# Moving the small q and output copies of a decode attention kernel from GpSimd to VectorE, with outputs laid out by tile

## The chip, the cores and the metric

The kernel runs on one core of one Trainium2 chip. The metric is device time in microseconds (us) from launch to end. The six runs of the kernel before span 0.22% (653.43 to 654.88 us), so differences below 0.3% are only read from repeated runs on the same chip. The trace of an execution starts and ends a little inside the device time: 652.1 us of trace belong to 653.5 us of time. A run counts as slow when it lies over 1.5% above the fastest of its kernel.

## The reference, cut to what matters

One decode step for 4 sequences: layer norm, grouped-query attention over a long cache, a gated MLP branch, and a residual.

```python
B, Sq, D = 4, 1, 448
Hq, Hkv, Sk, Dh = 16, 8, 8192, 256            # k_cache, v_cache: (B, Hkv, Sk, Dh), bfloat16
q = (x @ wq).reshape(B, Sq, Hq, Dh) ...
p = softmax(einsum(q, k) * Dh ** -0.5)
s = (p @ v) ... .reshape(B, Sq, Hq * Dh) @ wo
return x + s * g                              # g: silu of a small MLP (w3, w4)
```

The two caches are 4 x 8 x 8192 x 256 x 2 bytes = 134 MB each, and each element is used once. That is nearly all of the 279 MB that the kernel reads.

## The kernel before

Work goes in 32 tiles, one for each pair of a sequence and a key head (`NH = Bn * HKV`). For each tile one 4 MB transfer brings keys and one brings values. TensorE (PE) transposes the keys, VectorE (DVE) and ScalarE (ACT) copy the transposes to on-chip memory (SBUF), PE multiplies with q, then comes the softmax, and two tiles later the product with the values. Both caches are double buffered.

The loads go through one queue, in program order, and each waits until VectorE has said that its buffer is free:

```python
def where(h):
    return Bn - 1 - h // HKV, h % HKV          # batch 3 first, batch 0 last

def load_k(h):
    b, g = where(h)
    if h >= 2:
        sp.wait_ge(S["v_k"], h - 1)            # VectorE: keys of tile h-2 are used up
    sp.dma_start(kn_dst(h), A_k_cache[b, g]...)
def load_v(h):
    ...
    if h < NH - 1:
        sp.wait_ge(S["v_v"], h + 1)            # VectorE: values of tile h-2 are used up
        sp.dma_start(vflat[h % 2], ...)
...
for h in range(2, NH):
    load_k(h)
    load_v(h - 2)
```

GpSimd feeds q to each tile and puts each output in its place. Its addresses are Python constants, as its program is unrolled; VectorE runs a hardware loop of two tiles and so writes to `otmp` first:

```python
OT = sb("OT", [P, HKV, REP, NHALF, PQ], BF16)  # batch innermost: 32 columns lie side by side

def put(h):                                    # GpSimd
    b, g = where(h)
    gp.wait_ge(S["v_o"], h + 4)
    gp.tensor_copy(OT[:, g, :, :, b], otmp[:, h % 2]...).then_inc(S["g_p"], 1)
    ...
for h in range(NH):
    b, g = where(h)
    if h >= 2:
        gp.wait_ge(S["v_v"], h - 1)
    gp.tensor_copy(qc[:, h % 2], qT[:, b, g]).then_inc(S["g_q"], 1)
    if h >= 5:
        put(h - 5)
```

VectorE's end of a tile, and the output projection of the tail, which takes OT as PE weights:

```python
v.sem_inc(S["v_k"], 1)                         # keys free
f_rmax(h)                                      # row maximum; PE then transposes it
f_diag(h)                                      # global maximum, to PE
f_po(h - 2)                                    # first: v.sem_inc(S["v_v"], 1), values free

ins = pe.matmul(o_ps[...], OT[:, hq // REP, hq % REP, dh, :], wo_sb[...], ...)
```

The last pieces of `wo` are loaded after all keys and values, so the projection ends the kernel. `f_warm` matmuls, whose results are not used, fill PE's gaps in the tail.

Of the kernel before, what the change touches and what calls it, by code (L numbers as in the profile page):

```python
# [10 lines left out]
BF16 = dt.bfloat16  # L11

P = 128
# [42 lines left out]
def bass_recurrent_scan__gqa_block_cached__mixer_s_mlp__decode_kernel(  # L56
# [13 lines left out]
    Bn, Sq, D = A_x.shape  # L70
    _, HKV, SK, DH = A_k_cache.shape
    HD = A_wq.shape[1]
    HQ = HD // DH
    REP = HQ // HKV
# [11 lines left out]
    DQ, PQ = D // NDG, P // NQD  # L86
# [3 lines left out]
    NHALF = DH // P  # L90
    NKC = HD // P
    NH = Bn * HKV
# [20 lines left out]
    NLATE = sum(len(g) for g in LATE)  # L113
    NWARM = 14
    ROW_PAD = 192
    QW = HDH // NQD
    assert QW <= 512 and QW % P == 0 and NQC == NQD * (QW // P)

# [2 lines left out]


    def where(h):
        return Bn - 1 - h // HKV, h % HKV

    with ExitStack() as es:
        def sb(name, shape, dty):
            return es.enter_context(nc.sbuf_tensor(name, shape, dty))

        align = sb("align", [P, ROW_PAD], BF16)  # L130
        kn = sb("kn", [P, 2, NCH, DH], BF16)
# [3 lines left out]
        ident_f = sb("ident_f", [P, P], F32)  # L135
        ident_b = sb("ident_b", [P, P], BF16)
        ones_f = sb("ones_f", [P, P], F32)
        qT = sb("qT", [P, Bn, HKV, NHALF, REP], BF16)
        qc = sb("qc", [P, 2, NHALF, REP], BF16)
        otmp = sb("otmp", [P, 2, NHALF, REP], BF16)  # L140
        OT = sb("OT", [P, HKV, REP, NHALF, PQ], BF16)
        ou_f = sb("ou_f", [P, D], F32)
        selb = sb("selb", [P, PQ], F32)
        q_b = sb("q_b", [P, QW], BF16)
        pT = sb("pT", [P, 2, NCH * REP + PVW], BF16)
# [9 lines left out]
        rz = sb("rz", [P, 2, REP], F32)  # L155
# [25 lines left out]
        S = {n: es.enter_context(nc.semaphore(n)) for n in (  # L181
            ["dx", "dwq", "dw3", "dw4", "dwo", "dk0", "dk1", "dv0", "dv1", "dout", "pause"]
            + ["dvl%d" % i for i in range(NPIECE)] + ["dwl%d" % i for i in range(len(LATE))]
            + ["p_td", "p_ta", "p_sc", "p_m1", "p_m2", "p_m3", "p_tr", "p_ou", "p_pv", "p_x", "p_q", "p_h", "p_h2", "p_o"]
            + ["v_ev", "a_ev", "v_rmax", "v_diag", "v_neg", "v_ot", "a_exp", "g_q", "g_c",
               "v_s", "v_a", "v_qb", "p_qt", "v_h2", "p_hs", "v_k", "v_v", "v_po", "v_o", "g_o", "g_p", "g_f", "v_xT", "v_qT", "v_hT", "v_c", "v_w", "a_c", "v_out"])}


        vflat = [vb[:, i].rearrange("p c d -> p (c d)") for i in range(2)]
# [13 lines left out]
        o_ps = pst[0]  # L203
        ou_ps = pst[3]
        ol_ps = pst[1]

        def kn_dst(h):
            return kn[:, h % 2].rearrange("p c d -> p (c d)")
# [63 lines left out]
        def take(eng, name, n=1):  # L272
            return eng.wait_ge(S[name], n).then_inc(S[name], -n)  # L273

        NPI, NPC = 4, 12

        def prog_pool(gp):
            def put(h):
                b, g = where(h)
                gp.wait_ge(S["v_o"], h + 4)  # L280
                gp.tensor_copy(OT[:, g, :, :, b],
                               otmp[:, h % 2].rearrange("p dh r -> p r dh")
                               ).then_inc(S["g_p"], 1)
                gp.wait_ge(S["g_p"], h + 1)
                gp.sem_inc(S["g_o"], 1)

            c = _Chain(gp, S["g_c"])
            c(gp.memset(ident_f[:, :], 0.0))
            c(gp.memset(ident_b[:, :], 0.0))
            c.sync()  # L290
            for t in (ident_b, ident_f):
                c(gp.affine_select(out=t[:, :], in_=t[:, :], compare_op=ALU.not_equal, fill=1.0,
                                   base=0, pattern=[[-1, P]], channel_multiplier=1))
            c(gp.memset(ones_f[:, :], 1.0))
            c(gp.memset(diag[:, :], 0.0))
            c(gp.memset(sel[:, :, :].rearrange("p c n -> p (c n)"), 0.0))
            c(gp.memset(rz[:, :, :].rearrange("p s r -> p (s r)"), 1.0))
            gp.wait_ge(S["v_c"], 2)
            c(gp.memset(pT[:, :, :].rearrange("p s n -> p (s n)"), 0.0))
            for i in range(2):  # L300
                c(gp.memset(po[:, i], 0.0))
            c(gp.memset(OT[:].rearrange("p g r d b -> p (g r d b)"), 0.0))
            assert c.n == NPC
            gp.wait_ge(S["v_qT"], 1)
            for h in range(NH):
                b, g = where(h)
                if h >= 2:
                    gp.wait_ge(S["v_v"], h - 1)
                gp.tensor_copy(qc[:, h % 2], qT[:, b, g]).then_inc(S["g_q"], 1)  # L309
                if h >= 5:  # L310
                    put(h - 5)
            for h in range(NH - 5, NH - 3):
                put(h)
            gp.wait_ge(S["g_p"], NH - 3)
            gp.sem_inc(S["g_f"], 1)

        def evac(engine, h, j):
            take(engine, "p_td" if j in D_GROUPS else "p_ta")
# [44 lines left out]
        def prog_dve(v):  # L363
            c = _Chain(v, S["v_c"])
# [59 lines left out]
                c(v.memset(t[:, :], 0.0))  # L424
            c.sync()
            v.sem_inc(S["v_po"], 1)
            v.sem_inc(S["g_o"], 5)
            v.sem_inc(S["dv0"], 16)
            v.sem_inc(S["dv1"], 16)
            v.wait_ge(S["g_c"], NPC)  # L430
# [22 lines left out]
            for m in range(NQD):  # L453
                hh, dh = divmod(m, NHALF)
# [2 lines left out]
                    qt_ps[:, m * P:(m + 1) * P].rearrange("p (i n) -> p i n", i=NQD)[  # L457
                        :, :, 0:NHF * Bn].rearrange("p i (a b) -> p i a b", a=NHF)))
            c.sync()
            v.sem_inc(S["v_qT"], 1)  # L460
            v.wait_ge(S["a_c"], 5)
            c(v.tensor_scalar(gel_b[:, :], gel_b[:, :], 1.0, 0.5, op0=ALU.add, op1=ALU.mult))
            c.sync()
# [15 lines left out]
            def f_rmax(h):  # L479
                take(v, "p_sc")  # L480
                v.tensor_reduce(rmax[:, :], psc[h % 2][:, 0:NCH * REP].rearrange(  # L481
                    "p (k h) -> p h k", h=REP), AX.X, ALU.max).then_inc(S["v_rmax"], 1)

            def f_diag(h):
                take(v, "p_m1")
                v.tensor_reduce(gmax[:, :], psm[0:REP, 0:P], AX.X, ALU.max  # L486
                                ).then_inc(S["v_s"], 1)
                take(v, "v_s")
                v.tensor_scalar(diag[:, :], ident_f[0:REP, 0:REP], gmax[:, 0:1], -SCALE,
                                op0=ALU.mult, op1=ALU.mult).then_inc(S["v_diag"], 1)  # L490
# [7 lines left out]
                v.sem_inc(S["v_v"], 1)  # L498
                v.tensor_copy(po[:, slot], psv[:, 0:CP * DH]).then_inc(S["v_po"], 1)  # L499

            def f_ot(h, last=False, slot=0):
                o = P + (4 + slot * NHALF) * REP
                ot_src = psm[:, o:o + NHALF * REP].rearrange("p (a r) -> p a r", a=NHALF)
                b, g = where(h)
                dst = OT[:, g, :, :, b].rearrange("p r a -> p a r") if last else otmp[:, h % 2]
                v.tensor_tensor(dst, ot_src,
                                rz[:, h % 2, :].unsqueeze(1).broadcast_to([P, NHALF, REP]),
                                ALU.mult).then_inc(S["v_s"], 1)
                take(v, "v_s")

            def f_fin(h):
                take(v, "p_m3")
                take(v, "g_o")
                f_ot(h - 2)
                v.reciprocal(rz[:, h % 2, :], psm[:, P + REP:P + 2 * REP]
                             ).then_inc(S["v_s"], 1)
                take(v, "v_s")
                v.sem_inc(S["v_o"], 1)

            with nc.Fori(0, NH // 2, engines=[mybir.EngineType.DVE]):  # L520
                for h in range(2):
                    for j in range(NGR):
                        if j in D_GROUPS:
                            evac(v, h, j)
                        if j == J_BC + 1:
                            f_negb(h - 1)
                        if j == J_SUM + 2:
                            f_fin(h - 1)
                    v.sem_inc(S["v_k"], 1)
                    f_rmax(h)  # L530
                    f_diag(h)
                    f_po(h - 2)
            h = NH - 1
            f_negb(h)
            take(v, "p_m3")
            f_ot(h - 2, True)
            v.reciprocal(rz[:, h % 2, :], psm[:, P + REP:P + 2 * REP]).then_inc(S["v_s"], 1)
            take(v, "v_s")
            v.sem_inc(S["v_ot"], 1)
            f_po(h - 1, 1)  # L540
            take(v, "p_tr")
            f_ot(h - 1, True, 1)
            v.sem_inc(S["v_ot"], 1)
            take(v, "p_ou")
            v.tensor_copy(ou_f[:, :], ou_ps[:, 0:D]).then_inc(S["v_a"], 1)
# [1 line left out]
            b, g = where(h)  # L547
# [12 lines left out]
        def prog_pe(pe, xn_mark, xn2_mark):  # L560
# [60 lines left out]

            def f_s(h, j):
                if j == 0:
                    take(pe, "g_q")
                take(pe, "v_ev" if j in D_GROUPS else "a_ev")
                for t in range(TB):
                    kl, half = divmod(t, NHALF)
                    kk = GC * j + kl
                    ins = pe.matmul(psc[h % 2][:, kk * REP:(kk + 1) * REP],  # L629
                                    kT[:, j % RING, t * P:(t + 1) * P], qc[:, h % 2, half, :],  # L630
                                    start=(half == 0), stop=(half == NHALF - 1))
                if j == NGR - 1:
                    ins.then_inc(S["p_sc"], 1)
# [57 lines left out]
            h = NH - 1  # L691
# [40 lines left out]
            def finish():  # L732
                f_bc(h)
                take(pe, "dwo", 16)
                pe.wait_ge(S["g_f"], 1)
                f_ou(range(NLATE, HQ - 3 * REP))
                take(pe, "v_po")
                f_warm(4)
# [106 lines left out]
```

## Time and profile before

| | before |
|---|---|
| time, median of 6 runs | 653.65 us (653.43 to 654.88) |
| read from HBM | 279 MB, 428 GB/s over the span |
| queue q1 | 99.5% of the time of 16 DMA engines |
| busy share: PE, DVE, ACT, GpSimd | 85%, 42%, 39%, 2% |

From the page of the kernel before: busy us with share of the span; the clock granted to PE and the busy share of the DMA in 40 equal slices (9 is 90% or more); the queue. PEld is PE's loading of weights, POOL is GpSimd.

```profile
PE 553.9 (85%) x9937; PEld 473.0 (73%) x9937; DVE 274.7 (42%) x589; ACT 256.3 (39%) x364; POOL 13.7 (2%) x77
...
PEclk9699999887899888789977979897789988878989
DMA  9999999999999999999999999999999999999997
...
q1 hardware_dynamic: 12328, 278.99, 99.5%
```

Every slice but the last is full. A packet of 32,768 bytes takes 1.21 us in the packet records, and 16 of them run at a time: 433 GB/s. The other engines are less full. PE is busy 85% of the span and idle for 98 us; the next view shows that most of this is one wait.

The waits of the kernel before (engine, line, what ended the wait: total us, times, longest), and those of the load queue:

```profile
PEld pst L617 <- issue: 82.8, 30, 4.7
...
DVE gmax L486 <- DVEq L273: 35.6, 32, 2.0
```

```profile
SPq L232 <- DVEq L529: 458.2, 30, 38.3
SPq L240 <- DVEq L498: 133.6, 31, 18.0
```

L617 is the transposing of keys: PE stands still before it 30 times, 2.8 us on the mean, and 28 of these waits end 0.1 us after a key load has landed. ("issue" only says that the profile shows no releaser.) The load queue (SPq, the engine that issues the loads) waits for VectorE most of the time, but that does not mean that the DMA starves. The issue table (size, median us from issue to landing) answers that:

```profile
kn<-in_A_k_cache_dram SPq DMA_DIRECT2D x32, 4096.0 KB, 25.6
vb<-in_A_v_cache_dram SPq DMA_DIRECT2D x31, 4096.0 KB, 30.8
```

A 4 MB load needs 9.7 us at 433 GB/s but lands 25.6 us after its issue: the rest is earlier work in the queue.

GpSimd's groups (count, busy us, mean ns), and the end of the timeline (start us, us, and in brackets the idle time before):

```profile
L309 POOL COPY qc<-qT 128x4 bf16<-128x4 bf16 x32 | 5.9, 188 | 583.7 <-DVEq L498 568.2 <-DVEq L460 15.5
L281 POOL COPY OT<-otmp 128x4 bf16<-128x4 bf16 x29 | 5.9, 202 | 30.9 <-DVEq L518 30.9
```

```profile
648.24 0.91 PEld L716 LDWEIGHTS pst<-wo_sb,OT 128*32 128x32 bf16 x20 [0.38 <-issue]
...
649.38 0.14 PEld L716 LDWEIGHTS pst<-wo_sb,OT 128*32 128x32 bf16 x4 [0.23 <-issue]
```

So GpSimd does 12 us of copies in 652 us, and the output projection (L716) waits 0.23 us for the last piece of `wo` before its last four weight loads.

### The profile page before, as it was taken

To read this page: it belongs to the slowest core of one execution; us is meant where nothing else is said; L and a number is where in the kernel's file an instruction comes from. 1 tells how busy PE (TensorE), PEld (TensorE's weight loads), DVE (VectorE), ACT (ScalarE), POOL (GpSimd) and SP (SyncE) were. 2 spreads that over 40 slices of the span, in tenths; PEclk is the share of its full clock that TensorE was granted. 3 is DMA by queue.
4 is the path that set the end of the run, shared out by engine and by line. 5 is a ranking of instruction groups with operands and counts; after the bars stand their busy time and mean duration, and the time that the engine had idled before them with its cause. 6 is when DMAs were issued, how large, how long until landed. Compare 5 with 4: busy or idle time off the path is not lost. (4 is left out here: it accounts for less than half of the span.)

```text
span 652.1 us, 22855 instructions
## 1 busy us (share of the span) xinstructions
PE 553.9 (85%) x9937; PEld 473.0 (73%) x9937; DVE 274.7 (42%) x589; ACT 256.3 (39%) x364; POOL 13.7 (2%) x77
## 2 busy tenths in 40 slices
PE   2798997988888988888898878997888898888898
PEld 1476886876766887676787757777776698767685
DVE  7343554443443443344433434443344344334442
ACT  4143454443433444333443423444343344333340
POOL 2000000000000000000000000000000000000000
PEclk9699999887899888789977979897789988878989
DMA  9999999999999999999999999999999999999997
GB/s 375 441 416 440 425 440 428 438 428 436 432 424 444 422 446 420 446 422 444 424 440 428 440 426 440 424 440 428 430 438 426 442 424 444 424 442 426 440 425 299
DMA packets 12354, 279.14 MB, mean 428 GB/s; under 512 B 1204, under 2 KB 3256, under 8 KB 3768
## 3 DMA queue, kind: packets, MB, share of 16 engines
q1 hardware_dynamic: 12328, 278.99, 99.5%
q8 instruction: 7, 0.11, 0.1%
q14 instruction: 3, 0.02, 0.0%
q10 hardware_dynamic: 16, 0.01, 0.0%
HBM read 278.99 MB, written 0.00 MB: 428 GB/s over the span
## 5 line engine op out<-in xcount | busy, mean ns | idle before, releaser
L617 PE MATMUL pst<-ident_b,kn 128*128 128x128 bf16 x4096 | 344.9, 238 | 77.8 <-PEq L273 75.4
L324 ACT ACTIVATE kT<-pst 128x1024 bf16<-128x1024 bf16 x224 | 229.5, 1025 | 358.8 <-ACTq L273 357.8
L617 PEld LDWEIGHTS pst<-ident_b,kn 128*128 128x128 bf16 x4096 | 274.2, 107 | 83.5 <-issue 82.8
L322 DVE COPY kT<-pst 128x1024 bf16<-128x1024 bf16 x288 | 197.5, 692 | 260.2 <-DVEq L273 260.2
L629 PE MATMUL psc<-qc,kT 128*128 128x2 bf16 x4096 | 177.9, 164 | 0.0
L629 PEld LDWEIGHTS psc<-qc,kT 128*128 128x128 bf16 x4096 | 156.5, 97 | 28.5 <-issue 28.3
L668 PE MATMUL psv<-vb,pT 128*4 128x512 bf16 x1056 | 87.2, 381 | 1.4 <-issue 1.4
L647 PE MATMUL psm<-sel,po 128*128 128x2 f32 x272 | 36.8, 257 | 0.5 <-PEq L273 0.5
L647 PEld LDWEIGHTS psm<-sel,po 128*128 128x128 f32 x272 | 34.8, 196 | 0.9 <-issue 0.9
L668 PEld LDWEIGHTS psv<-vb,pT 128*4 128x4 bf16 x1056 | 22.3, 82 | 16.8 <-issue 2.5
L481 DVE TENSOR_REDUCE rmax<-psc 128x2 f32<-128x128 f32 x32 | 9.3, 292 | 49.9 <-DVEq L273 49.9
L499 DVE COPY po<-psv 128x512 f32<-128x512 f32 x34 | 23.5, 692 | 3.0 <-DVEq L273 2.3
L486 DVE TENSOR_REDUCE gmax<-psm 2x1 f32<-2x128 f32 x32 | 8.9, 279 | 35.6 <-DVEq L273 35.6
L346 ACT ACTIVATE pT<-psc,negb 128x64 bf16<-128x64 f32 x66 | 20.7, 333 | 5.4 <-ACTq L273 5.4
L641 PEld LDWEIGHTS psm<-diag,ones_f 2*128 2x128 f32 x66 | 13.9, 260 | 6.4 <-issue 5.2
L309 POOL COPY qc<-qT 128x4 bf16<-128x4 bf16 x32 | 5.9, 188 | 583.7 <-DVEq L498 568.2
L641 PE MATMUL psm<-diag,ones_f 2*128 2x2 f32 x66 | 16.6, 318 | 1.1 <-PEq L273 0.9
L346 ACT ACTIVATION_READ_ACCUMULATOR pT<-psc,negb 128x1 f32 x66 | 13.6, 206 | 0.0
L637 PEld LDWEIGHTS psm<-ident_f,rmax 128*2 128x2 f32 x32 | 2.6, 80 | 14.4 <-issue 14.4
L659 PE MATMUL psm<-rowsum,ones_f 128*128 128x2 f32 x64 | 11.6, 251 | 0.0
L565 PE MATMUL pst<-ident_b,xn_b 4*128 4x4 bf16 x14 | 0.6, 161 | 11.3 <-DVE xn_b L394 6.7
L659 PEld LDWEIGHTS psm<-rowsum,ones_f 128*128 128x128 f32 x64 | 9.5, 188 | 0.0
(101 smaller groups left out, 111.0 us busy)
## 6 DMA issues: line engine op xcount, KB each, us to landing
kn<-in_A_k_cache_dram SPq DMA_DIRECT2D x32, 4096.0 KB, 25.6
vb<-in_A_v_cache_dram SPq DMA_DIRECT2D x31, 4096.0 KB, 30.8
vb<-in_A_wq_dram SPq DMA_DIRECT2D x1, 3584.0 KB, 11.3
vb<-in_B_w_dram SPq DMA_DIRECT2D x2, 1568.0 KB, 16.2
wo_sb<-in_A_wo_dram SPq DMA_DIRECT2D x1, 2688.0 KB, 43.4
kn<-in_A_v_cache_dram SPq DMA_DIRECT2D x1, 2048.0 KB, 25.9
kn<-in_A_v_cache_dram SPq DMA_DIRECT2D x1, 1024.0 KB, 27.9
kn<-in_A_v_cache_dram SPq DMA_DIRECT2D x2, 512.0 KB, 29.1
```

The source lines that it names most:

```text
L322: engine.tensor_copy(dst, src).then_inc(S["v_ev"], 1)
L324: engine.activation(dst, src, ACT.Copy).then_inc(S["a_ev"], 1)
L346: ins = act.activation(pv_p[:, :, hh], sc[:, :, hh], ACT.Exp, bias=negb[:, s, hh:hh + 1], scale=SCALE, accum_out=rowsum[:, s, hh:hh + 1])
L481: v.tensor_reduce(rmax[:, :], psc[h % 2][:, 0:NCH * REP].rearrange("p (k h) -> p h k", h=REP), AX.X, ALU.max).then_inc(S["v_rmax"], 1)
L486: v.tensor_reduce(gmax[:, :], psm[0:REP, 0:P], AX.X, ALU.max).then_inc(S["v_s"], 1)
L499: v.tensor_copy(po[:, slot], psv[:, 0:CP * DH]).then_inc(S["v_po"], 1)
L617: ins = pe.transpose(dst[:, t * P:(t + 1) * P], kn[:, h % 2, GC * j + kl, half * P:(half + 1) * P], ident_b[:, :])
L629: ins = pe.matmul(psc[h % 2][:, kk * REP:(kk + 1) * REP], kT[:, j % RING, t * P:(t + 1) * P], qc[:, h % 2, half, :], start=(half == 0), st ...
L641: pe.matmul(psm[:, P:P + REP], ones_f[0:REP, :], diag[:, :], start=True, stop=True).then_inc(S["p_m2"], 1)
L647: ins = pe.matmul(dst(dh)[:, 0:width], po[:, slot, i * DH + dh:(i + 1) * DH:NHALF], sel[:, i, 0:width], start=(i == 0), stop=(i == CP - 1))
L659: pe.matmul(psm[:, P + REP:P + 2 * REP], ones_f[:, :], rowsum[:, h % 2, :], start=True, stop=True)
L668: ins = pe.matmul(psv[o:o + CP * REP, 0:CP * DH], pT[:, h % 2, kk * REP:(kk + CP) * REP], src[:, kk:kk + CP, :].rearrange("p c d -> p (c d)"),
```

## The change

GpSimd is taken out of the loop. VectorE's loop counts in elements (`at`), and its instructions address OT and q through that register. OT is laid out by tile and batches run from 0 up, so that the loop's one counter steps evenly through both q and OT. The intent is fewer hand-overs between engines: one operation in place of a write to `otmp`, a semaphore and a GpSimd copy.

```diff
     def where(h):
-        return Bn - 1 - h // HKV, h % HKV
+        return h // HKV, h % HKV
...
-        otmp = sb("otmp", [P, 2, NHALF, REP], BF16)
-        OT = sb("OT", [P, HKV, REP, NHALF, PQ], BF16)
+        OT_all = sb("OT_all", [P, OT_AHEAD * TW + PQ * HKV * TW], BF16)
...
+        OT = OT_all[:, OT_AHEAD * TW:].rearrange("p (b g d r) -> p g r d b", g=HKV, d=NHALF, r=REP)
...  (GpSimd: put(h) and the loop over tiles removed)
-            v.sem_inc(S["v_qT"], 1)
+            v.tensor_copy(qc[:].rearrange("p s d r -> p (s d r)"), qT_all[:, 0:2 * TW]
+                          ).then_inc(S["v_q"], 2)
...
+            def f_q(at, s):
+                v.tensor_copy(qc[:, s].rearrange("p d r -> p (d r)"),
+                              qT_all[:, bass.ds(at, TW)]).then_inc(S["v_q"], 1)
...
-            with nc.Fori(0, NH // 2, engines=[mybir.EngineType.DVE]):
+            with nc.Fori(0, NH * TW, 2 * TW, engines=[mybir.EngineType.DVE]) as at:
...
-                            f_fin(h - 1)
+                            f_fin(h - 1, at + h * TW)
                     v.sem_inc(S["v_k"], 1)
                     f_rmax(h)
+                    f_q(at + (h + 2) * TW, h)
                     f_diag(h)
                     f_po(h - 2)
...  (PE waits on v_q in place of g_q, and no longer on g_f)
```

More of the change, by code (lines that the diff above doesn't have):

```diff
@@ L115, in bass_recurrent_scan__gqa_block_cached__mixer_s_mlp__decode_kernel @@
     ROW_PAD = 192
+    TW = NHALF * REP
+    OT_AHEAD = 3
     QW = HDH // NQD
@@ L137, in bass_recurrent_scan__gqa_block_cached__mixer_s_mlp__decode_kernel @@
         ones_f = sb("ones_f", [P, P], F32)
-        qT = sb("qT", [P, Bn, HKV, NHALF, REP], BF16)
+        qT_all = sb("qT_all", [P, (NH + 4) * TW], BF16)
         qc = sb("qc", [P, 2, NHALF, REP], BF16)
-        otmp = sb("otmp", [P, 2, NHALF, REP], BF16)
-        OT = sb("OT", [P, HKV, REP, NHALF, PQ], BF16)
+        OT_all = sb("OT_all", [P, OT_AHEAD * TW + PQ * HKV * TW], BF16)
         ou_f = sb("ou_f", [P, D], F32)
@@ L184, in bass_recurrent_scan__gqa_block_cached__mixer_s_mlp__decode_kernel @@
             + ["p_td", "p_ta", "p_sc", "p_m1", "p_m2", "p_m3", "p_tr", "p_ou", "p_pv", "p_x", "p_q", "p_h", "p_h2", "p_o"]
-            + ["v_ev", "a_ev", "v_rmax", "v_diag", "v_neg", "v_ot", "a_exp", "g_q", "g_c",
-               "v_s", "v_a", "v_qb", "p_qt", "v_h2", "p_hs", "v_k", "v_v", "v_po", "v_o", "g_o", "g_p", "g_f", "v_xT", "v_qT", "v_hT", "v_c", "v_w", "a_c", "v_out"])}
+            + ["v_ev", "a_ev", "v_rmax", "v_diag", "v_neg", "v_ot", "a_exp", "v_q", "g_c",
+               "v_s", "v_a", "v_qb", "p_qt", "v_h2", "p_hs", "v_k", "v_v", "v_po", "v_xT", "v_hT", "v_c", "v_w", "a_c", "v_out"])}
         vflat = [vb[:, i].rearrange("p c d -> p (c d)") for i in range(2)]
@@ L205, in bass_recurrent_scan__gqa_block_cached__mixer_s_mlp__decode_kernel @@
         ol_ps = pst[1]
+        qT = qT_all[:, 0:NH * TW].rearrange("p (b g d r) -> p b g d r", b=Bn, d=NHALF, r=REP)
+        OT = OT_all[:, OT_AHEAD * TW:].rearrange("p (b g d r) -> p g r d b", g=HKV, d=NHALF,
+                                                 r=REP)
         def kn_dst(h):
@@ L273, in take @@
             return eng.wait_ge(S[name], n).then_inc(S[name], -n)
-        NPI, NPC = 4, 12
+        NPI, NPC = 4, 13
         def prog_pool(gp):
-            def put(h):
-                b, g = where(h)
-                gp.wait_ge(S["v_o"], h + 4)
-                gp.tensor_copy(OT[:, g, :, :, b],
-                               otmp[:, h % 2].rearrange("p dh r -> p r dh")
-                               ).then_inc(S["g_p"], 1)
-                gp.wait_ge(S["g_p"], h + 1)
-                gp.sem_inc(S["g_o"], 1)
             c = _Chain(gp, S["g_c"])
@@ L301, in prog_pool @@
                 c(gp.memset(po[:, i], 0.0))
-            c(gp.memset(OT[:].rearrange("p g r d b -> p (g r d b)"), 0.0))
+            c(gp.memset(qT_all[:, NH * TW:], 0.0))
+            c(gp.memset(OT_all[:, :], 0.0))
             assert c.n == NPC
-            gp.wait_ge(S["v_qT"], 1)
-            for h in range(NH):
-                b, g = where(h)
-                if h >= 2:
-                    gp.wait_ge(S["v_v"], h - 1)
-                gp.tensor_copy(qc[:, h % 2], qT[:, b, g]).then_inc(S["g_q"], 1)
-                if h >= 5:
-                    put(h - 5)
-            for h in range(NH - 5, NH - 3):
-                put(h)
-            gp.wait_ge(S["g_p"], NH - 3)
-            gp.sem_inc(S["g_f"], 1)
         def evac(engine, h, j):
@@ L426, in prog_dve @@
             v.sem_inc(S["v_po"], 1)
-            v.sem_inc(S["g_o"], 5)
             v.sem_inc(S["dv0"], 16)
@@ L499, in f_po, with f_ot, f_fin @@
                 v.tensor_copy(po[:, slot], psv[:, 0:CP * DH]).then_inc(S["v_po"], 1)
-            def f_ot(h, last=False, slot=0):
+            def f_ot(at, s, slot=0):
                 o = P + (4 + slot * NHALF) * REP
                 ot_src = psm[:, o:o + NHALF * REP].rearrange("p (a r) -> p a r", a=NHALF)
-                b, g = where(h)
-                dst = OT[:, g, :, :, b].rearrange("p r a -> p a r") if last else otmp[:, h % 2]
+                dst = OT_all[:, bass.ds(at, TW)].rearrange("p (a r) -> p a r", a=NHALF)
                 v.tensor_tensor(dst, ot_src,
-                                rz[:, h % 2, :].unsqueeze(1).broadcast_to([P, NHALF, REP]),
+                                rz[:, s, :].unsqueeze(1).broadcast_to([P, NHALF, REP]),
                                 ALU.mult).then_inc(S["v_s"], 1)
                 take(v, "v_s")
-            def f_fin(h):
+            def f_q(at, s):
+                v.tensor_copy(qc[:, s].rearrange("p d r -> p (d r)"),
+                              qT_all[:, bass.ds(at, TW)]).then_inc(S["v_q"], 1)
+            def f_fin(h, at):
                 take(v, "p_m3")
-                take(v, "g_o")
-                f_ot(h - 2)
+                f_ot(at, h % 2)
                 v.reciprocal(rz[:, h % 2, :], psm[:, P + REP:P + 2 * REP]
@@ L517, in f_fin @@
                 take(v, "v_s")
-                v.sem_inc(S["v_o"], 1)
-            with nc.Fori(0, NH // 2, engines=[mybir.EngineType.DVE]):
+            with nc.Fori(0, NH * TW, 2 * TW, engines=[mybir.EngineType.DVE]) as at:
                 for h in range(2):
@@ L535, in prog_dve @@
             take(v, "p_m3")
-            f_ot(h - 2, True)
+            f_ot((h - 2 + OT_AHEAD) * TW, h % 2)
             v.reciprocal(rz[:, h % 2, :], psm[:, P + REP:P + 2 * REP]).then_inc(S["v_s"], 1)
@@ L541, in prog_dve @@
             take(v, "p_tr")
-            f_ot(h - 1, True, 1)
+            f_ot((h - 1 + OT_AHEAD) * TW, 1 - h % 2, 1)
             v.sem_inc(S["v_ot"], 1)
@@ L623, in f_s @@
                 if j == 0:
-                    take(pe, "g_q")
+                    take(pe, "v_q")
                 take(pe, "v_ev" if j in D_GROUPS else "a_ev")
@@ L734, in finish @@
                 take(pe, "dwo", 16)
-                pe.wait_ge(S["g_f"], 1)
                 f_ou(range(NLATE, HQ - 3 * REP))
```

## The prediction

> **What bounds the kernel now.** The DMA. In the page's 40 slices the DMA row reads 9 everywhere but the last (7); the queue table gives q1 279 MB and 99.5% of the time of 16 engines. Packets of 32 KB take 1.21 us, 16 at a time: 32,768 B x 16 / 1.21 us = 433 GB/s[...]. PE is busy 85% and waits some 80 us for keys (waits view, transposes' weight loads, 30 waits), DVE 42%, ACT 39%, GpSimd 2%.
>
> The queue is never short. A 4,096 KB load takes 9.7 us at that rate but lands 25.6 us (keys) and 30.8 us (values) after its issue, so some 16 us of earlier work lies ahead of it. DVE's releases would have to come 16 us later before the DMA ran dry. Every load in the loop is released by DVE, none by GpSimd.
>
> **Removed.** GpSimd: 32 copies of q (188 ns) and 29 of outputs to OT (202 ns), 12 us in all, with their semaphores. All off the critical path.
>
> **Added.** DVE: 32 copies of q, 128x4; the negb copy of 128x2 takes 150 ns, so I estimate 100 to 190 ns each, in a gap: between the row maximum and the global maximum DVE idles 35.6 us / 32 = 1.1 us per tile. Register addresses on 64 instructions[...]. Writing an output stays one operation (152 ns). At worst values are released 0.1 to 0.3 us later per tile, against 16 us of slack. In the head the first copy of q delays hT by about 0.15 us, but PE then runs 14 warming matmuls and waits for the first keys: absorbed.
>
> **Moved.** The batches are read from 0 up rather than from 3 down: same bytes and packets, no effect. OT is laid out by tile, so PE's weight load of 32 columns reads with a step of 64 bytes. [...] It touches only 44 weight loads in the tail, 97 ns each now. There the 20 output matmuls at 648.27 us run 57 ns apart, then the weight loads idle 0.23 us for the last piece of wo, then 4 matmuls and two DVE operations end the chain. If each strided load cost 20 ns more, 16 of them cost 0.3 us, of which 0.1 us would show. The last write of OT becomes contiguous (175 to about 150 ns), inside the same slack.
>
> **Sum.** Steady state 0; head 0; tail -0.05 to +0.3 us: 653.7 us. 8 in 10: 652.8 to 655.0 (the three runs before span 653.44 to 654.88). Chances: faster by over 2% 0.01, within 2% 0.98, slower by over 2% 0.01.
>
> **What the profile would show.** DMA row still 9s, q1 at 99.5%; GpSimd with memsets only; DVE with 32 small copies in the idle time before the global maximum, which falls accordingly; keys landing about 25 us after issue; PE's waits for keys about 80 us; last bytes at about 648.4 us; OT weight loads in the tail at 97 ns if the step is free.
>
> **What would make it wrong.** If register-addressed DVE instructions stalled DVE for microseconds, so that PE fell behind the loads (PE waits only 2.6 us per tile); if the order of batches changed the rate of HBM; if strided weight loads were several times slower.

What is marked as cut in it, and in some of the expectations below, are statements that no trace of this case shows. Here they are a comparison of the 433 GB/s with a figure from elsewhere, a rule for reads with a step, and a guess for the cost of register addresses. That guess was one term of the 0.1 to 0.3 us by which values would be released later; against 16 us of slack it entered the sum as 0. The sum came to 653.7 us: the time before, with 0 for the steady state, 0 for the head and -0.05 to +0.3 us for the tail. The 20 ns per strided load in the tail are an assumption of mine, not read from a trace.

## More of the kernel before

By the packet records the last packet of `wo` ends at 648.93 us.

## The result

| | before | after |
|---|---|---|
| time, median of 6 runs | 653.65 us (653.43 to 654.88) | 654.25 us (653.33 to 655.4) |
| 278 of the 279 MB had landed at | 645.37 us | 645.39 us |
| last packet of `wo` ended at | 648.93 us | 648.79 us |
| GpSimd busy | 13.7 us | 3.6 us |
| DVE busy | 274.7 us | 276.9 us |

The ratio of the times is 1.0003, with a 95% interval of 0.9989 to 1.0017: no difference. Ratios here are the mean time of one kernel's fast runs over that of the other's of the same rounds, so not quite the ratio of the medians. The two rows of landing times are worked out from the packet records of the two traces.

The page of the new kernel:

```profile
PE 550.5 (84%) x9937; PEld 470.7 (72%) x9937; DVE 276.9 (42%) x622; ACT 255.8 (39%) x364; POOL 3.6 (1%) x17
...
PEclk9998999888799898889987888988779987978999
DMA  9999999999999999999999999999999999999997
...
q1 hardware_dynamic: 12328, 278.99, 99.5%
```

Its waits and its issue table:

```profile
PEld pst L604 <- issue: 86.6, 31, 4.7
...
DVE gmax L471 <- DVEq L278: 32.3, 32, 1.0
```

```profile
kn<-in_A_k_cache_dram SPq DMA_DIRECT2D x32, 4096.0 KB, 25.5
vb<-in_A_v_cache_dram SPq DMA_DIRECT2D x31, 4096.0 KB, 30.5
```

GpSimd's copies are gone, the DMA row is the same, and loads land as long after their issue as before. The new copies of q stand in VectorE's timeline at the end of each tile; the first one in the loop:

```profile
43.90 0.29 DVE L466 TENSOR_REDUCE rmax<-psc 128x2 f32<-128x128 f32 x1 [1.50 <-DVEq L278]
44.11 0.16 DVE L496 COPY qc<-qT_all 128x4 bf16 x1
45.27 0.28 DVE L471 TENSOR_REDUCE gmax<-psm 2x1 f32<-2x128 f32 x1 [1.01 <-DVEq L278]
```

From the row maximum to the global maximum there are 1.37 us; before there were 1.38 us (43.75 to 45.13 us). The copy (158 ns) lies in time that VectorE spends waiting for PE; the wait fell from 35.6 us to 32.3 us in total. Register addresses cost nothing that can be seen: the copy starts before the row maximum ends, and the write of an output takes 152 ns with one as it did without.

One thing did get slower, in the tail: each weight load of the last projection. The end of the new kernel's timeline, the same from 649.2 us on, and the records of the OT weight loads there (duration ns, least/median/most), before and after:

```profile
648.11 1.35 PEld L703 LDWEIGHTS pst<-wo_sb,OT_all 128*32 128x32 bf16 x24 [0.50 <-issue]
...
649.24 0.23 PEld L703 LDWEIGHTS pst<-wo_sb,OT_all 128*32 128x32 bf16 x4
```

```profile
L716 PEld LDWEIGHTS pst<-wo_sb,OT x24: 92/97/97, 648.2 to 649.4; 128*32 128x32 bf16 x24
```

```profile
L703 PEld LDWEIGHTS pst<-wo_sb,OT_all x24: 131/134/157, 648.1 to 649.3; 128*32 128x32 bf16 x24
```

A load takes 134 ns in place of 97. The loads overlap, though. In the single records they start in pairs, and pairs follow each other every 96 ns in both kernels; only the second of a pair starts later, some 33 ns after the first in place of 17. From the first to the twentieth start there are 0.85 us, before 0.81 us. And the last four still wait for the last piece of `wo`: it landed at 649.27 us before and at 649.13 us after (the semaphore's time), and these loads start 0.11 us later in both, at 649.38 and 649.24 us. In the new kernel the idle time before them is 0.14 us, too short for the view to list it as a wait. From the first of these matmuls to the end of the last, the chain of waits has 1.52 us before (648.27 to 649.79) and 1.55 us after (648.14 to 649.69).

### The profile page after: what moved, and what is told of

Read it like the earlier page. It is cut to its first block, busy times and chain, and to the rows that moved or that the text cites. A ratio compares the mean times of both kernels' runs of the same rounds, so it can differ in the third digit from the quotient of the medians.

```text
span 652.0 us, 22813 instructions
## 1 busy us (share of the span) xinstructions
PE 550.5 (84%) x9937; PEld 470.7 (72%) x9937; DVE 276.9 (42%) x622; ACT 255.8 (39%) x364; POOL 3.6 (1%) x17
## 5 line engine op out<-in xcount | busy, mean ns | idle before, releaser
L655 PE MATMUL psv<-vb,pT 128*4 128x512 bf16 x1056 | 85.6, 378 | 0.0
L471 DVE TENSOR_REDUCE gmax<-psm 2x1 f32<-2x128 f32 x32 | 8.9, 279 | 32.3 <-DVEq L278 32.3
L331 ACT ACTIVATION_READ_ACCUMULATOR pT<-psc,negb 128x1 f32 x66 | 13.6, 206 | 0.0
L474 DVE TENSOR_SCALAR diag<-ident_f,gmax 2x2 f32<-2x2 f32 x32 | 6.9, 217 | 4.8 <-DVEq L278 1.1
```

What stands on the lines that cost most here:

```text
L331: ins = act.activation(pv_p[:, :, hh], sc[:, :, hh], ACT.Exp, bias=negb[:, s, hh:hh + 1], scale=SCALE, accum_out=rowsum[:, s, hh:hh + 1])
L471: v.tensor_reduce(gmax[:, :], psm[0:REP, 0:P], AX.X, ALU.max).then_inc(S["v_s"], 1)
L655: ins = pe.matmul(psv[o:o + CP * REP, 0:CP * DH], pT[:, h % 2, kk * REP:(kk + CP) * REP], src[:, kk:kk + CP, :].rearrange("p c d -> p (c d)"),
```

## The experiments

Three theories:

1. The DMA sets the pace. What the change removes and adds lies in time that the queue of pending loads hides.
2. VectorE's release of buffers is on the critical path (as the 458 us wait of the load queue could suggest), and the change happens to leave it alone.
3. The change has effects on the engines, a gain and a loss that cancel.

### How late may a release be? (delay8, delay17)

GpSimd, idle now, hands on the release of the key buffers, after some memsets into a tile that nobody reads. From tile 6 on.

```diff
+            for h in range(6, NH):                       # GpSimd
+                gp.wait_ge(S["v_k"], h - 1)
+                for i in range(8):                       # delay17: 17
+                    gp.memset(idle[:, :], 0.0).then_inc(S["g_i"], 1)
+                    take(gp, "g_i")
+                gp.sem_inc(S["g_k"], 1)
...  (load_k, from tile 6 on)
-                    sp.wait_ge(S["v_k"], h - 1)
+                    sp.wait_ge(S["g_k"], h - 5)
```

> The new kernel, but from tile 6 on the release of a key buffer reaches the load queue only after GpSimd has run 8 memsets of 128x1024 bf16 (961 ns each in the trace of the new kernel, so 8 to 9 us late with their semaphores). Theory 1 (the 16 DMA engines set the pace, and some 14 us of earlier transfers lie in the queue when a key load is issued): unchanged within the noise, 653 to 656 us, while the wait between issue and the first packet falls from about 14 us to about 6 us. Theory 2 (the release of buffers by DVE is on the critical path, so that a DVE stream that is a little quicker or slower shows): each buffer is used every second tile, so about 8 us for each of 13 pairs of tiles, over 100 us slower.

> As delay8 with 17 memsets, 17 to 18 us late, more than the some 14 us of queued work. Theory 1: the queue now runs dry once per tile; late by the excess of 3 to 6 us for each of 13 pairs of tiles, 40 to 80 us slower, 690 to 735 us, and the DMA row falls to 8. Theory 2: over 220 us slower, twice the loss of delay8. If nothing happens at all, the reading of the queue is wrong.

Measured (one run each, state unknown; before 654.56 us on the same chip): delay8 654.74 us, delay17 732.91 us. In delay8 the wait from issue to first packet fell from 13.9 us in the new kernel to 4.8 us, so the delay of 9.1 us was really there, in 26 tiles, and cost nothing. In delay17 that wait was 0.96 us, the same in tile after tile: the queue was empty, the slack used up. The issue tables of delay8 and delay17:

```profile
kn<-in_A_k_cache_dram SPq DMA_DIRECT2D x32, 4096.0 KB, 16.7
...
kn<-in_A_k_cache_dram SPq DMA_DIRECT2D x32, 4096.0 KB, 12.4
```

The DMA row of delay8 (first) is as full as before, that of delay17 has holes:

```profile
DMA  9999999999999999999999999999999999999996
...
DMA  9999997997989978989988899989899897998997
```

and PE's waits for keys double:

```profile
PEld pst L614 <- issue: 162.6, 30, 8.5
```

This kernel is 78 us slower, at the upper end of the 40 to 80 us that theory 1 expected. An estimate from these numbers comes close: 17 memsets at 9.1 / 8 us are 19.3 us, the slack is 13.9 - 0.96 = 13 us, and 13 pairs of tiles lose the rest, 82 us. Theory 2 is dead: it wanted over 100 us from delay8. A release of keys may be some 9 us late for nothing (from tile 6 on; the earlier tiles, with less in the queue, were not delayed); the change moved it by a fraction of one microsecond.

### Eight times the added work (after_q8)

```diff
             def f_q(at, s):
+                for i in range(7):
+                    v.tensor_copy(qjunk[:, i], qT_all[:, bass.ds(at, TW)]).then_inc(S["v_s"], 1)
+                    take(v, "v_s")
```

> The new kernel with the copy of q done 8 times per tile in place of once (7 of them into a tile that nobody reads), to make the added VectorE work 8 times as large: 7 more copies of 158 ns with a semaphore each, about 1.3 to 1.6 us per tile, 45 us in all. Theory 1: unchanged, 653 to 656 us, as the releases have 14 us to spare. Theory 3 (the removed GpSimd work was worth something and the added DVE work gives it back, so that the two cancel): about 40 us slower.

Measured: 655.68 us, before 654.56 us (one run each). Not 40 us, but not quite nothing; a single run cannot tell 1.1 us from its spread. The copies do not fit into VectorE's own gap: with their semaphores the seven take 2.05 us, and from the row maximum to the global maximum there are 2.55 us in every tile in place of 1.37. What hides this is the queue of loads. It is taken up again below.

### The order of the batches alone (before_order)

The kernel before, with only `where` changed to `return h // HKV, h % HKV`.

> The kernel before with nothing changed but the order of the batches: keys and values are read from batch 0 up, as in the new kernel. Theory 1: same bytes, same packets, same rate; within 0.2% of the kernel before, 427 to 429 GB/s over the span. If the order of addresses mattered to HBM, the 32 KB packets would take other than 1.21 us and the time would move by more than 0.3%, which could have hidden an opposite effect of the rest of the change.

Measured in 5 rounds: 653.81 us, ratio 0.9997 (0.9984 to 1.0011). The mean time of a 32 KB packet is 1.2135 us in both traces. The order is worth nothing, and hid nothing.

### Without the limit of the DMA (before_quarter_v, after_quarter_v)

Both kernels with three quarters of most value loads left out. The values are wrong. (The comparison with the reference still passes, so in this problem it says little about the attention branch.)

```diff
-                    sp.dma_start(vflat[h % 2], src.rearrange("p c d -> p (c d)")
+                    sp.dma_start(vflat[h % 2][:, 0:NCH // 4 * DH],
+                                 src[:, 0:NCH // 4, :].rearrange("p c d -> p (c d)")
```

> The kernel before with 31 of the 32 value loads cut to their first quarter (the result is wrong on purpose: the rest of each values buffer is stale), so 97.5 MB of 279 MB are not read. This takes the DMA limit away: the rest would take some 420 us at 433 GB/s. Theory 1 expects PE to set the pace now; where keys were early (tiles 3 to 5 of the trace) tiles followed each other in 14.9 us, so some 500 to 580 us[...], and a DMA row of 6 to 9. If the time stays near 650 us, the DMA was not the limit.

> The new kernel with the same cut, wrong on purpose too: what the change is worth once the DMA no longer hides the engines. Theory 1 with my reading of the VectorE gaps (the copy of q falls into a wait for PE that is 1 us long): within 0.5% of before_quarter_v. Theory 3 (the change does save or cost engine time, hidden by the DMA): a difference of more than 1%, that is 5 us or more, in either direction.

Measured in 3 rounds: 530.77 us (528.37 to 532.12) and 530.89 us (530.83 to 532.02). Against the kernel before that is 0.8114 and 0.8127. The page of before_quarter_v:

```profile
PE 505.2 (95%) x9937; PEld 427.5 (81%) x9937; DVE 269.7 (51%) x589; ACT 253.9 (48%) x364; POOL 13.6 (3%) x77
...
PEclk9999899999999999999999999999999999999999
DMA  9999688898888888898887889888888888988580
```

Taking bytes away saves 123 us, so bytes were the limit. Now PE is: it is busy 95% of the span. The page of after_quarter_v:

```profile
PE 505.8 (96%) x9937; PEld 428.1 (81%) x9937; DVE 272.1 (51%) x622; ACT 254.3 (48%) x364; POOL 3.8 (1%) x17
```

And in this other regime, too, the two kernels are equal, within 0.12 us of median (the runs of each spread over 1 to 4 us, so smaller effects would not show). Theory 3 wanted 5 us or more. So the change is not a hidden gain that waits for a faster DMA. This comparison alone could still hide a gain and a loss of equal size. With the DMA's limit in place after_q8 speaks against that: seven more copies per tile cost 1 to 3 us there (below), so the one that the change adds costs well under 1 us by my estimate and cannot be paying back a gain. In the quarter kernels the added part was not varied alone.

### The step of the weight loads (ot_step64, ot_step16, ot_step8)

The kernel before, GpSimd and all, with OT in another order in memory. The view that the code uses stays the same.

```diff
-        OT = sb("OT", [P, HKV, REP, NHALF, PQ], BF16)
+        OT_mem = sb("OT_mem", [P, PQ * HKV * REP * NHALF], BF16)
+        OT = OT_mem[:, :].rearrange("p (b g r d) -> p g r d b", ...)     # ot_step64
+        OT = OT_mem[:, :].rearrange("p (g b r d) -> p g r d b", ...)     # ot_step8
         # ot_step16: "p (y b x r d) -> p y x r d b" with x=2, and g split into (y, x)
```

> The kernel before with nothing changed but the order of OT in memory: tile outermost, so that the output projection's weight loads read their 32 columns with a step of 64 bytes, as in the new kernel; GpSimd still writes it. If the step is what lengthened these loads from 97 to 134 and 142 ns, they take 134 to 142 ns here; if it was the producer or the address, they stay at 97 ns. Time unchanged, 653 to 656 us, in both cases.

> The kernel before with OT ordered so that the output projection's weight loads read with a step of 16 bytes. [...] these loads are as slow as with 64 bytes, 131 to 142 ns; if it grows with the step, they lie between 97 and 131 ns. Time unchanged, 653 to 656 us.

> The same with a step of 8 bytes[...]: 92 to 97 ns, as contiguous. If any step slows the load, over 105 ns. Time unchanged, 653 to 656 us.

The weight loads of the last projection in the three (duration ns, least/median/most), step 64, 16 and 8 bytes:

```profile
L717 PEld LDWEIGHTS pst<-wo_sb,OT_mem x24: 131/133/154, 648.7 to 649.8; 128*32 128x32 bf16 x24
```

```profile
L717 PEld LDWEIGHTS pst<-wo_sb,OT_mem x24: 134/136/158, 648.3 to 649.5; 128*32 128x32 bf16 x24
```

```profile
L717 PEld LDWEIGHTS pst<-wo_sb,OT_mem x24: 105/107/126, 648.8 to 650.0; 128*32 128x32 bf16 x24
```

Contiguous loads take 97 ns, a step of 8 bytes 107, of 16 bytes 136, of 64 bytes 133. The step alone does it; who wrote OT plays no part (at 64 bytes 133 ns after GpSimd's writes, 134 ns after VectorE's). From 16 to 64 bytes it does not grow; what causes the cost was not shown. That a step of 8 bytes would be free was a miss, if a small one: 107 ns is not 97, and just over the 105 ns from which my expectation counted a load as slowed. Times: 653.95, 653.64 and 654.07 us in single runs, unchanged.

### Where work is exposed (after_again, after_q8_again, after_tail7)

The 1.1 us of after_q8 was left. One more kernel runs seven extra copies only once, in the last tile:

```diff
             h = NH - 1
+            for i in range(7):
+                v.tensor_copy(qjunk[:, i], qT_all[:, 0:TW]).then_inc(S["v_s"], 1)
+                take(v, "v_s")
             f_negb(h)
```

> The new kernel unchanged, on the same chip as the two runs that follow, to compare them with. 653.3 to 655.4 us as before, median about 654.

> after_q8 once more, in rounds: its single time of 655.68 us was 1.1 us above the kernel before, where theory 1 said zero and theory 3 said 40. New form of theory 1: the extra VectorE work of tiles 0 to 30 costs nothing, but that of tile 31, after which no more DMA work hides anything, costs its 1.2 us less the slack of the tail (0.2 to 1.6 us by the clock granted to the last tile). So 0 to 1.5 us above after_again. If it is 0 within the interval, the 1.1 us was the spread of single runs.

> The new kernel with seven extra small VectorE copies run once only, after the loop and ahead of the copy of negb of the last tile (some 2.0 us in series). By the new form of theory 1 this alone costs as much as or more than the seven copies in each of 32 tiles: 0.5 to 2 us above after_again. If only the sum of VectorE work mattered, it would cost 1/32 of what after_q8 costs, nothing that can be seen.

| 5 rounds, before 654.0 us | median (lowest to highest) | ratio, 95% interval |
|---|---|---|
| after_again | 654.35 us (653.39 to 654.56) | 1.0000 (0.9987 to 1.0013) |
| after_q8_again, 7 copies in each of 32 tiles | 655.75 us (654.34 to 660.28) | 1.0047 (1.0026 to 1.0069) |
| after_tail7, 7 copies once | 657.8 us (655.62 to 658.95) | 1.0056 (1.0042 to 1.007) |

So the extra copies do cost something, and 7 of them in the last tile cost no less than 224 in all tiles (the intervals overlap). The two do not stand at the same place of the tile: in the traces the last tile's chain on VectorE is held up by 1.2 us in after_q8_again and by 2.3 us in after_tail7. That the tiles before cost nothing is seen more directly in the packet records: 278 MB had landed at 645.31 us in after_q8 and at 645.44 us in after_q8_again, against 645.37 and 645.39 us in the kernels before and after and 645.72 us in after_again. So what VectorE does in tiles 0 to 30 is free here, what it does after the last keys is not, as then no load waits behind. In its size I was wrong: the 2.05 us that the seven copies take cost 3.3 us in the means (657.49 against 654.15 us) where I had allowed 2.

PE's clock comes into that. The granted clock in the records is full or half, in pieces that are multiples of 3.41 us. The windows view of three traces, along those pieces (start to end; length; busy us of PE, PEld, DVE, ACT, POOL; granted clock; DMA share; GB/s): after_q8, after_q8_again, after_tail7.

```profile
632.70:636.10 3.40, 1.35 (x19) 0.36 (x13) 2.09 (x12) 0.00 (x0) 0.00 (x0) 1.00 0.86 371
636.10:639.50 3.40, 3.34 (x19) 1.56 (x19) 0.79 (x2) 0.70 (x4) 0.00 (x0) 0.50 1.02 439
```

```profile
631.83:635.24 3.41, 2.39 (x41) 0.94 (x38) 1.37 (x8) 0.00 (x0) 0.00 (x0) 1.00 0.94 404
635.24:638.65 3.41, 2.31 (x23) 1.60 (x23) 1.44 (x6) 0.70 (x4) 0.00 (x0) 1.00 0.96 413
```

```profile
636.00:639.40 3.40, 1.54 (x18) 1.47 (x22) 0.59 (x4) 0.70 (x4) 0.00 (x0) 1.00 1.00 429
639.40:642.80 3.40, 3.40 (x37) 1.78 (x27) 0.23 (x2) 0.00 (x0) 0.00 (x0) 0.51 0.96 405
```

In after_q8 and after_q8_again PE waits the same 2.11 us for VectorE. In the first the wait falls into one window, PE is busy 1.35 of 3.4 us, and the next window runs at half the clock. In the second the wait is split over two windows, PE is busy 2.3 us in each, and the clock stays full; the traced spans are 654.2 and 652.9 us. All pieces of a trace lie on one grid of 3.41 us (to within 1 ns in the traces of the kernels before and after), and the grid differs from trace to trace: counted from the start of the span it begins at 1.55 us in the first of these two and at 0.83 us in the second. The same kernel lost the clock here in one run, after_q8, and kept it in another, after_q8_again. How busy PE was in the window ahead of one at half clock varies: 1.35 us in after_q8, 1.54 us in after_tail7, and 1.42 us in the trace of the kernel before (616.0 to 619.4 us). In all 14 traces (from 22 us on), each of the 216 full-clock windows with PE busy for less than 1.5 us was followed by half the clock, of the 146 with 1.5 to 2.2 us 81 were, and of the 1,677 with more only 4, so busy time alone gives no sharp limit. In the trace of the kernel before a half-clock window (619.4 to 622.8 us) fell into the transposing of the last keys, in that of the new kernel none did: its last row maximum came at 631.47 us, the other's at 633.06 us. That cost nothing: the traces end within 0.1 us of each other, as both kernels then wait for the last piece of `wo`.

This is shown for the traced runs. What made the slower untraced ones is open, as they have no record of windows. One window as above explains some 1.3 us (654.2 against 652.9), not the 660.28 us of the slowest.

## Why the prediction was right, point by point

- **"What bounds the kernel now. The DMA."** Right. Three quarters of the values taken away saved 123 us; 9 us of delay in each release of keys from tile 6 on cost nothing, a longer one 78 us.
- **"some 16 us of earlier work lies ahead of it"**. Right in kind. The packet records give 13.6 us (and 2.6 to 10.4 us in tiles 2 to 5, which I had overlooked). My 16 us came from landing times less 9.7 us of transfer; but a key load takes longer than that even with an empty queue, 12.4 us in delay17 (median).
- **Removed: "All off the critical path"**. Right: the time is the same without GpSimd's copies, and neither what was added nor what was moved can be paying for them (after_q8, before_order, ot_step64). In the quarter kernels the times are equal too.
- **Added: 100 to 190 ns per copy of q, in a gap of 1.1 us.** Right: 158 ns, and the distance from the row maximum to the global maximum stayed at 1.37 us. A cost of register addresses does not show at all: the write of an output takes 152 ns with and without.
- **Head: hT some 0.15 us later, absorbed.** In the trace hT starts at 20.39 us where it was 20.27 us, and the first 5 MB, 18 MB and 50 MB land at the same time within 0.1 us.
- **Moved: the order of batches has "no effect"**. Right, ratio 0.9997.
- **The step of 64 bytes: an assumed 20 ns per load, "of which 0.1 us would show"**. Both sizes were off. A load takes 37 ns more, but as pairs of loads follow each other every 96 ns in both kernels, and the last four wait for `wo` in both, the chain of the projection grew by 0.03 us only. In the quarter kernels, where it does not wait for `wo`, it is 1.43 us before and 1.46 us after, again 0.03 us.
- **Not foreseen:** where the spread of 1 to 2 us between runs comes from. The traces show two sources: the last packet of `wo` ended at 648.7 to 649.2 us in most (delay17 and the quarter kernels left aside) but at 649.97 us in that of after_again, whose 32 KB packets took 1.2141 us on the mean in place of 1.2134 to 1.2138; and half-clock windows in the last tile delay PE, which is so close behind the DMA there that it can end last. In the traces of delay8, ot_step64 and ot_step8 two such windows lie between 616.5 and 624.7 us; their last chain runs through PE's products and not through the wait for `wo`, and the last projection starts at 648.8 to 649.5 us, where it was 648.3 us before. How often each happens is open. The range of 652.8 to 655.0 us was taken from the spread of the runs before, without knowing its cause; one of the new kernel's six runs (655.4 us) lay above it.

No version that beats both kernels came out of this. The last packet ends at 648.8 us of a span of 652.0 us, so only some 3 us (0.5%) come after the last transfer of inputs, and the bytes are all needed.

## What to carry to other kernels

When an issuer waits for an engine, ask how much work lies in the queue at that moment before calling the wait critical: bytes issued earlier, over the rate, give the slack, and a delay put in on purpose checks it. If the DMA row is full everywhere and the queue never runs empty, work taken off the engines inside the loop can be worth nothing, as here, while work in the last tile, after the last keys, can cost its full length or more (3.3 us for 2.05 us here). Equal times can also hide two effects that cancel, so run both versions once with the limit taken away, and enlarge the added part alone.
